# An attention-and-feed-forward kernel on one core: the scaled decay rows of the later blocks move from VectorE to ScalarE, and two small steps change their place

## The chip, the cores and the metric

The kernel runs on one core of one Trainium2 chip. The metric is the device time of one execution in microseconds. The core has engines that run side by side, each through its own instructions in order: PE (TensorE, matrix products, with PEld for its weight loads), DVE (VectorE), ACT (ScalarE), POOL (GpSimd) and SP (SyncE, which here only issues transfers). Transfers are issued by SP, ACT or POOL and carried out by 16 DMA engines. Engines wait for one another through semaphores.

## The reference

Two stages are fused. The first is a state-space attention with a decay per token, over 4 batches, 8 heads, 768 tokens, 32 channels per head and 16 state channels; the second a bilinear feed-forward with 256 model channels and 1536 inner ones.

```python
# per chunk of 32 tokens
cum = np.cumsum(la, axis=-1)                                   # la = log of the decay a
L = np.exp(cum[:, :, :, None] - cum[:, :, None, :]) * causal
y_intra = einsum('bhij,bhjd->bhid', einsum(Cc, Bc) * L, xc)
y_inter = einsum('bhin,bhnd->bhid', Cc, state) * exp(cum)[..., None]
state = exp(sum(la)) * state + sum_j Bx_j * exp(cum[-1] - cum[j])
...
a = x @ w_a; b = x @ w_b                                       # x: tokens x 256
out = (a * b) @ w_out
```

## The kernel before

The sequence is cut into 6 blocks of 128 tokens rather than chunks of 32. A *pair* is one block of two batches, so there are 12 pairs, numbered block by block (0 and 1 are block 0, 2 and 3 block 1, and so on); pairs 0 to 3 are handled one by one ("early", `P0` = 4), the later ones in groups of a block.

**Decays.** `a_sb` holds the decay of the 32 batch-and-head rows by block. `scan` makes `Pr`, the running product of the decay within a block; `over_mid` makes `rmid`, one over the product at the middle token. `Ps` holds `Pr` times `rmid` for the four later blocks (2 to 5). From it come the factors by which B and C are scaled: `late_factors` transposes `Ps` on VectorE into `fCl`, and `spread_rows` copies the last three blocks of `Ps` through DRAM (`rows`, one transfer) into `Pq` (four transfers), from which `block_factors` makes `fCq`. The small steps on `hr`, `hs`, `hsx` turn the decay products into G, the decay that carries the state from one block to the next: a small matrix product with `hsx` (L921) writes it to PSUM and ScalarE copies it out (L924). `maskbd` is a constant mask, cast on ScalarE (L903), that `state_spread` on POOL uses for the states of the pairs 0 and 1.

**Attention of a pair.** B and C are scaled (`scale_bc`), transposed on PE, and multiplied into four PSUM banks (`scores`). VectorE multiplies them by the causal mask for three quarters, and for the fourth, ScalarE copies it to `tmp` (L491) and POOL multiplies (L492). `pv` (or `pv_u` within `group` for the later pairs, matmuls of L500) multiplies the masked scores with x, and the result is copied to X2T or XB.

**Feed-forward.** A `unit(p, k2)` multiplies X2T of a pair by a part of `w_a` (tile `aps`) and of `w_b` (`bps`), ScalarE copies `aps` to `asb` (L711), and `times` on VectorE multiplies `bps` by `asb` into `hk` (L718). `out_mm` multiplies `hk` by `Wo`. Pair 0's first three units are written apart (`units_mm`, tiles `aps` and `bps`, with three `times` behind them); `go` runs units whole.

**What sets the order.** The schedule is written by hand: each engine runs its instructions in the order of the program text, and the framework adds the waits. The feed-forward's products and some others take one of four PSUM banks, in the order of the string `BANKS`: a product has to wait until the last reader of what lay in its bank has finished. Around the change the banks are: `bps` of pair 0's units in 1, 2, 0; unit (1,0) in 3 (`aps`) and 1 (`bps`); unit (1,1) in 3 and 2; unit (1,2) in 0 and 3; then the two `aps` of the units (0,3) and (0,4) in 1 and 0. Transfers issued by SP likewise go out in program order; those behind `spread_rows` are b, c and x of pair 3, then the loads of the later pairs (`loads_bc`, `loads_x`, `load_block`), then the first stores. The four transfers to `Pq` wait until `rows` has landed.

Of the kernel before, what the change touches and what calls it, by code (L numbers as in the profile page):

```python
# [14 lines left out]
ALU = mybir.AluOpType  # L15
# [14 lines left out]
def kernel(  # L30
# [13 lines left out]
    nc = tc.nc  # L44

    nb, H, S, D = x.shape
    N = B.shape[-1]
    Q = 128
# [5 lines left out]
    BH = nb * H  # L54
    NBP = nb // 2
    NP = NBP * NBLK
    NG = NBLK - 1
    P0 = 4
# [22 lines left out]
    headm = ch[:, 0:H]  # L81
# [13 lines left out]
    maskbd = big.tile([128, H, D], f16, name="maskbd")  # L95
    warm = big.tile([128, 128], f16, name="warm")
    causal_q = big.tile([128, Q], f16, name="causal_q")
    Pr = big.tile([BH, NBLK, Q], f32, name="Pr")
    rmid = big.tile([BH, NBLK], f32, name="rmid")
# [5 lines left out]
    NL = NBLK - P0 // NBP  # L105
    Ps = big.tile([BH, NL, Q], f32, name="Ps")
# [31 lines left out]
    def bank(name):  # L138
        return psf.tile([128, 512], f32, name=name, tag=f"ff{next(banks)}")
# [79 lines left out]
    def load_wo(half):  # L219
        return nc.gpsimd.dma_start(  # L220
            Wo[:, 6 * half : 6 * half + 6].rearrange("p (g kk) e -> p g (kk e)", kk=3),
            moe_w_out.rearrange("(g p kk) e -> p g (kk e)", p=128, kk=3)[:, 2 * half : 2 * half + 2],
        )

    nc.sync.dma_start(a_sb, a.rearrange("b h (k q) -> (b h) k q", q=Q))
    for p_ in range(3):
# [22 lines left out]
        out=ident, in_=ident, compare_op=ALU.is_equal, fill=0.0, base=0, pattern=[[-1, 128]], channel_multiplier=1  # L249
    )  # L250
    for bt in range(2):
        v = causal[64 * bt : 64 * bt + 64]
        nc.gpsimd.affine_select(
            out=v, in_=v, compare_op=ALU.is_ge, fill=0.0, base=0, pattern=[[-1, 2], [1, Q]], channel_multiplier=-2
# [26 lines left out]
    def over_mid(lo, hi):  # L281
        nc.vector.reciprocal(rmid[:, lo:hi], Pr[:, lo:hi, 63])
# [33 lines left out]
    def f_c(k):  # L316
        return fC[:, k, H : H + 64].rearrange("p (r b t h) -> p r b t h", r=2, b=NBP, t=2)[:, :, :, 0]

    def late_rows(eng):
        k0 = P0 // NBP  # L320
        eng.tensor_tensor(
            out=Ps, in0=Pr[:, k0:], in1=rmid[:, k0:].unsqueeze(2).broadcast_to((BH, NL, Q)), op=ALU.mult
        )

    def last_factors():
        nc.vector.reciprocal(fBq, fCq[:, NT - 1, :, 0 : 2 * nb])
# [5 lines left out]
    def spread_rows(eng):  # L332
        rows = far.tile([BH, NT, Q], f32, name="rows")
        eng.dma_start(rows, Ps[:, NL - NT :])
        for m in range(4):
            eng.dma_start(
                Pq[32 * m : 32 * m + 2 * nb],
                rows.rearrange("(b h) k q -> b h (k q)", h=H)[:, 2 * m : 2 * m + 2],
            )
# [185 lines left out]
    def ds_mm(p, c0, banks):  # L525
        s = st[p]
        s["DS"] = [b_[:, c0 : c0 + 2 * D] for b_ in banks]
        for bt, m in itertools.product(range(2), range(4)) if p >= P0 else ():
            nc.tensor.matmul(
                s["DS"][bt][32 * m : 32 * m + 32, :],  # L530
                s["bm"][:, bt, 2 * m : 2 * m + 2, :].rearrange("p h n -> p (h n)"),
                by_token(s["X16"])[:, bt, 2 * m : 2 * m + 2].rearrange("p h d -> p (h d)"),
                start=True,
                stop=True,
                skip_group_check=True,
                tile_position=(0, 32 * m),
            )
        for r in range(2) if p < P0 else ():
            for m in range(4):
                for bt in range(2):  # L540
                    k = slice(64 * bt, 64 * bt + 64)
                    nc.tensor.matmul(
                        s["DS"][bt][32 * m : 32 * m + 32, :],
                        s["bm"][k, r, 2 * m : 2 * m + 2, :].rearrange("p h n -> p (h n)"),
                        s["X16"][k, 2 * m : 2 * m + 2, r, :],
                        start=(r == 0),
                        stop=(r == 1),
                        skip_group_check=True,
                        tile_position=(64 * bt, 32 * m),
                    )  # L550
# [92 lines left out]
    def state_sums(p, bts=(0, 1)):  # L643
        blk, bp = divmod(p, NBP)
        for bt in bts:
            g = G[:, 2 * bp + bt, blk : blk + 1]
            ds = st[p]["DS"][bt]
            if blk == 0:
                nc.vector.tensor_scalar(U32[:, p, bt], ds, g, None, ALU.mult)
            else:  # L650
                nc.vector.scalar_tensor_tensor(
                    out=U32[:, p, bt], in0=ds, scalar=g, op0=ALU.mult, in1=gU[:, p % (2 * NBP), bt], op1=ALU.add
                )
# [43 lines left out]
    def units_mm(p, k2s, W, ps, f, ks):  # L697
        for j in ks:
            k2, t_, kk = k2s[j // 2], ps[j // 2], j % 2
            nc.tensor.matmul(  # L700
                t_[:, kk * 2 * Q : (kk + 1) * 2 * Q],
                w_up(W, 2 * k2 + kk, f),
                X2T[:, p, :, f],
                start=(f == 0 and kk == 0),
                stop=(f == 1),
                skip_group_check=True,
            )

    def evac_a(a_ps, on_dve=False):
        asb = ffh.tile([128, 512], f32, name="asb", tag="asb", bufs=5)  # L710
        (nc.vector.tensor_copy if on_dve else nc.scalar.copy)(asb, a_ps)  # L711
        return asb

    def times(p, k2, b_ps, asb):
        s = st[p]
        if "hk" not in s:
            s["hk"] = ffh.tile([128, NK, 2 * Q], f16, name="hk", tag="hk")
        nc.vector.tensor_tensor(  # L718
            out=s["hk"][:, 2 * k2 : 2 * k2 + 2, :].rearrange("p k q -> p (k q)"), in0=b_ps, in1=asb, op=ALU.mult
        )  # L720

    def unit(p, k2, between=None):
        a_ps = unit_mm(p, k2, Wa)
        asb = evac_a(a_ps)
        if between:
            between()
        b_ps = unit_mm(p, k2, Wb)
        return lambda: times(p, k2, b_ps, asb)
# [89 lines left out]
    def fb(k):  # L818
        if k * NBP >= P0:
            nc.vector.reciprocal(fBl[:, 0 : NL - 1], fCl[:, 0 : NL - 1])  # L820
        else:
            nc.vector.reciprocal(fB[:, k], f_c(k))

    def go(*items):
        for p, k2 in items:
            unit(p, k2)()

    def pull(p):
# [33 lines left out]
        out=causal_q, in_=causal_q, compare_op=ALU.is_ge, fill=0.0, base=0, pattern=[[1, Q]], channel_multiplier=-1  # L862
# [18 lines left out]
    asb = [evac_a(aps[0])]  # L881
# [4 lines left out]
    scan(2, 3)  # L886
    scan(5, NBLK)
    over_mid(2, NBLK)
    late_rows(nc.vector)
    spread_rows(nc.sync)  # L890
    for w in range(2):
        for bt in range(2):
            load1(nc.gpsimd, 2, w, bt)
# [1 line left out]
    for bt in range(2):  # L895
        load1(nc.gpsimd, 2, 2, bt)
    tiles(3)
    bps = [bank("bps") for _ in range(3)]
# [1 line left out]
    pv(1)  # L900
    units_mm(0, range(3), Wb, bps, 0, range(4, 6))
    units_mm(0, range(3), Wb, bps, 1, range(6))
    nc.scalar.copy(maskbd, headm.unsqueeze(2).broadcast_to((128, H, D)))  # L903
    times(0, 0, bps[0], asb[0])
    nc.vector.tensor_tensor(out=hr, in0=Pr[:, 0:NG, Q - 1], in1=rmid[:, 0:NG], op=ALU.mult)
    nc.vector.tensor_tensor(out=hs, in0=hr, in1=Pr[:, 1:NBLK, 63], op=ALU.mult)
    nc.vector.tensor_tensor(
        out=hsx[0:BH],
        in0=hs.unsqueeze(1).broadcast_to((BH, nb, NG)),
        in1=selb.rearrange("p (b g) -> p b g", b=nb),  # L910
        op=ALU.mult,
    )
    times(0, 1, bps[1], asb[1])
    times(0, 2, bps[2], asb[2])
    fb(1)
    scale_bc(2, 0, nc.gpsimd)
    scale_bc(2, 1, nc.gpsimd)
    load_wo(1)
    go((1, 0), (1, 1))
    gps = SC[0][:, 256 : 256 + nb * NG]  # L920
    nc.tensor.matmul(gps, indm, hsx.rearrange("p b g -> p (b g)"), start=True, stop=True, skip_group_check=True)  # L921
    for p in range(NBP):
        ds_mm(p, 2 * D * p, SC[:2])
    nc.scalar.copy(G.rearrange("p b g -> p (b g)"), gps)  # L924
    go((1, 2))
    state_sums(0)
    state_sums(1)
# [9 lines left out]
    asb = [evac_a(t_) for t_ in aps]  # L937
# [235 lines left out]
```

## Time and profile before

| what | value |
| --- | --- |
| time, median of 3 runs | 124.03 us (124.01 to 124.08) |
| time of the profiled execution | 123.79 us |
| its span (first to last instruction) | 122.0 us |
| granted TensorE clock, mean | 0.998 |
| PE busy | 117.0 us (96% of the span), 1440 matmuls |
| DVE busy | 93.2 us (76%), 186 instructions |
| ACT busy | 76.4 us (63%), 157 instructions |
| POOL busy | 63.3 us (52%), 86 instructions |
| bytes moved by DMA | 12.25 MB |

Times in the views are microseconds from the start of the span unless marked ns. L12 is line 12 of the kernel; a helper's line stands for all its calls. A timeline row gives start, length, engine, line, operation, the tile written and the tiles read, and how many instructions were merged (x8); in brackets, how long the engine had been idle before and what ended that. In the rows of groups the three fields behind the count are: busy time and mean ns of one; idle time of the engine before them. "SPq" is the issue of a transfer on SP, not its flight. The ends of matmuls are modelled.

### The profile page before, as it was taken

The page shows a single profiled execution, that of the slowest core. Times are in us where ns is not written, and L with a number is a line of the kernel's source. Part 1 is how long each engine was busy: PE and PEld are TensorE (multiplying, and loading weights), DVE is VectorE, ACT ScalarE, POOL GpSimd, SP SyncE. Part 2 cuts the span into 40 slices and gives each one's busy share as a digit, 9 for nine tenths or more (in the row PEclk, how much of TensorE's full clock was granted, in tenths as well). Part 3 has the DMA queues.
Part 4 walks back from the last instruction along what each step waited for, and adds up shares of the span by engine and source line. Part 5 has one row for each costly group of instructions (what it writes and reads, how often), then busy time and mean ns, then how long its engine had stood idle before and what let it go on. Part 6 is the DMA issues. An engine that isn't in the chain of part 4 may idle for free.

```text
span 122.0 us, 3714 instructions
## 1 busy us (share of the span) xinstructions
PE 117.0 (96%) x1440; PEld 79.3 (65%) x1440; DVE 93.2 (76%) x186; ACT 76.4 (63%) x157; POOL 63.3 (52%) x86
## 2 busy tenths in 40 slices
PE   6999899999999999999999999999999999999990
PEld 2345689889898798645476464766464784555890
DVE  4999999895886979699985999996898444847100
ACT  0458856937669865987659657767666737566220
POOL 7997987493883994077998089219044000000000
PEclk9999999999999999999999999999999999999999
DMA  3999999986987297299329961011101012010122
GB/s 62 181 169 207 196 205 209 141 146 84 101 118 121 59 94 130 46 130 131 73 51 206 327 208 43 0 51 43 43 0 43 5 43 86 0 43 5 43 88 84
DMA packets 44593, 12.25 MB, mean 100 GB/s; under 512 B 39296, under 2 KB 44128, under 8 KB 44576
## 3 DMA queue, kind: packets, MB, share of 16 engines
q1 hardware_dynamic: 40000, 7.53, 32.0%
q0 software_dynamic: 2304, 4.06, 17.8%
q10 hardware_dynamic: 2272, 0.43, 1.8%
q8 instruction: 11, 0.18, 0.6%
q14 instruction: 6, 0.05, 0.1%
HBM read 11.18 MB, written 3.19 MB: 118 GB/s over the span
## 4 chain that ended last, share of the span: by engine, by line
PE 86%; DVE 5%; ACT 3%; DMA 2%; issue 1%; DVEq 0%
PE ops L790 18%; PE aps L765 17%; PE bps L765 16%; PE ops L733 9%; PE bps L687 8%; PE aps L687 8%; PE SC L440 2%; DVE t L494 2%; PE SC L500 2%; DMA a_sb<-in_a_dram 2%; PE SC L455 1%; ACT asb L711 1%; PE aps L700 1%; PE tr L406 1%; PE SC L590 1%
## 5 line engine op out<-in xcount | busy, mean ns | idle before, releaser
L711 ACT COPY asb<-aps 128x512 f32<-128x512 f32 x72 | 42.0, 588 | 14.2 <-PE aps L765 9.5
L775 DVE TENSOR_TENSOR hkb<-bps,asb 128x512 f16<-128x512 f32 x48 | 32.0, 687 | 10.5 <-ACT asb L711 10.0
L765 PE MATMUL aps<-XB,Wa 128*128 128x512 f16 x96 | 28.6, 379 | 0.1
L765 PE MATMUL bps<-XB,Wb 128*128 128x512 f16 x96 | 28.5, 379 | 0.0
L790 PE MATMUL ops<-Wo,hkb 128*128 128x256 f16 (+1 forms) x204 | 22.6, 266 | 0.0
L790 PEld LDWEIGHTS <-hkb 128*128 128x128 f16 x204 | 18.5, 98 | 3.0
L494 DVE TENSOR_TENSOR t<-SC,causal_q 128x512 f16<-128x512 f32 x24 | 15.5, 682 | 3.2 <-PE SC L440 3.2
L718 DVE TENSOR_TENSOR hk<-bps,asb 128x512 f16<-128x512 f32 x24 | 15.8, 681 | 2.0 <-ACT asb L711 2.0
L765 PEld LDWEIGHTS <-Wb 128*128 128x128 f16 x96 | 9.9, 103 | 10.9
L492 POOL TENSOR_TENSOR t<-tmp,causal_q 128x512 f16<-128x512 f32 x8 | 9.3, 1159 | 14.5 <-ACT tmp L491 14.2
L765 PEld LDWEIGHTS <-Wa 128*128 128x128 f16 x96 | 9.7, 103 | 9.2 <-issue 0.3
L365 POOL TENSOR_SCALAR x<-xn 128x512 f16<-128x512 f32 x8 | 11.9, 1489 | 3.9 <-DMA xn<-in_x_dram 2.1
L802 ACT ACTIVATE osb<-ops 128x256 f32<-128x256 f32 (+1 forms) x16 | 6.0, 377 | 11.3 <-PE ops L790 11.2
L687 PE MATMUL bps<-X2T,Wb 128*128 128x256 f16 x84 | 12.4, 272 | 0.1
L687 PE MATMUL aps<-X2T,Wa 128*128 128x256 f16 x84 | 12.5, 273 | 0.0
L733 PE MATMUL ops<-Wo,hk 128*128 128x256 f16 x96 | 11.6, 273 | 0.0
L733 PEld LDWEIGHTS <-hk 128*128 128x128 f16 x96 | 9.0, 98 | 1.2
L687 PEld LDWEIGHTS <-Wb 128*128 128x128 f16 x84 | 8.6, 103 | 0.9 <-issue 0.3
L687 PEld LDWEIGHTS <-Wa 128*128 128x128 f16 x84 | 8.3, 104 | 1.1 <-issue 0.2
L494 DVE TENSOR_TENSOR t<-SC,causal 128x512 f16<-128x512 f32 x13 | 8.2, 682 | 0.8 <-PE SC L455 0.6
L491 ACT COPY tmp<-SC 128x512 f32<-128x512 f32 x11 | 6.5, 595 | 1.9 <-PE SC L440 1.1
L267 PE MATMUL SC<-warm 128*128 128x512 f16 (+1 forms) x14 | 5.5, 551 | 1.0 <-POOL warm L238 1.0
(110 smaller groups left out, 136.3 us busy)
## 6 DMA issues: line engine op xcount, KB each, us to landing
out_dram<-osb SPq DMA_DIRECT2D x23, 128.0 KB, 1.7
xn<-in_x_dram SPq DMA_DIRECT2D x5, 256.0 KB, 4.6
Wo<-in_moe_w_out_dram POOLq DMA_DIRECT2D x2, 384.0 KB, 5.4
bn<-in_B_dram SPq DMA_DIRECT2D x6, 128.0 KB, 4.4
rq<-in_C_dram SPq DMA_DIRECT2D x24, 32.0 KB, 2.6
xn<-in_x_dram POOLq DMA_DIRECT2D x3, 256.0 KB, 4.8
Wa<-in_moe_w_a_dram POOLq DMA_DIRECT2D x2, 192.0 KB, 4.9
xn<-in_x_dram SPq DMA_DIRECT2D x3, 128.0 KB, 5.9
```

The costliest lines, as they stand in the source:

```text
L365: eng.tensor_scalar(xo, xi, XS, None, ALU.mult)
L491: nc.scalar.copy(tmp, i_)
L492: nc.gpsimd.tensor_tensor(out=o_, in0=tmp, in1=c_, op=ALU.mult)
L494: nc.vector.tensor_tensor(out=o_, in0=i_, in1=c_, op=ALU.mult)
L687: nc.tensor.matmul(ps[:, kk * 2 * Q : (kk + 1) * 2 * Q], w_up(W, k, f), X2T[:, p, :, f], start=(f == 0), stop=(f == 1), skip_group_check=True,
L711: (nc.vector.tensor_copy if on_dve else nc.scalar.copy)(asb, a_ps)
L718: nc.vector.tensor_tensor(out=s["hk"][:, 2 * k2 : 2 * k2 + 2, :].rearrange("p k q -> p (k q)"), in0=b_ps, in1=asb, op=ALU.mult)
L733: nc.tensor.matmul(o_ps[:, 0:d_model], hk[:, k, bt * Q : (bt + 1) * Q], Wo[:, k, :], start=(k == 0), stop=(k == NK - 1), skip_group_check= ...
L765: nc.tensor.matmul(t_, w_up(W, k, f), XB[:, blk - P0 // NBP, f].rearrange("p t j q -> p (t j q)"), start=(f == 0), stop=(f == 1), skip_gro ...
L775: return lambda: nc.vector.tensor_tensor(out=s["hk"][:, k], in0=ps[1], in1=asb, op=ALU.mult)
L790: nc.tensor.matmul(o_ps[:, 0:w], hk[:, k, c * Q : (c + 1) * Q], Wo[:, k, cs], start=(k == 0), stop=(k == NK - 1), skip_group_check=True,)
L802: nc.scalar.activation(out=o_sb[:, 0:w], in_=o_ps[:, 0:w], func=AF.Copy, scale=1.0 / (YS * YS))
```

## The change

The helper `late_rows` no longer makes all four blocks' rows of `Ps` in one VectorE operation (32x512). It now makes one block's rows at a time (32x128), on ScalarE, by a multiplication with a scale per partition, for the blocks in a given range. Its calls are spread: the rows 1 and 2 where the cast of `maskbd` stood, ahead of the first `times` of pair 0; row 3 between the units (1,0) and (1,1), with `spread_rows` (the SP transfers, which need the rows 1 to 3) right behind it; row 0 behind ScalarE's copy of G. The cast of `maskbd` follows there. On VectorE the second and third `times` of pair 0 come ahead of `hr`, `hs` and `hsx`.

```diff
-    def late_rows(eng):
-        k0 = P0 // NBP
-        eng.tensor_tensor(
-            out=Ps, in0=Pr[:, k0:], in1=rmid[:, k0:].unsqueeze(2).broadcast_to((BH, NL, Q)), op=ALU.mult
-        )
+    def late_rows(lo, hi):
+        for k in range(lo, hi):
+            r = P0 // NBP + k
+            nc.scalar.mul(Ps[:, k], Pr[:, r], rmid[:, r : r + 1])
...
     over_mid(2, NBLK)
-    late_rows(nc.vector)
-    spread_rows(nc.sync)
     for w in range(2):
...
     units_mm(0, range(3), Wb, bps, 1, range(6))
-    nc.scalar.copy(maskbd, headm.unsqueeze(2).broadcast_to((128, H, D)))
+    late_rows(1, 3)
     times(0, 0, bps[0], asb[0])
+    times(0, 1, bps[1], asb[1])
+    times(0, 2, bps[2], asb[2])
     nc.vector.tensor_tensor(out=hr, in0=Pr[:, 0:NG, Q - 1], in1=rmid[:, 0:NG], op=ALU.mult)
...
-    times(0, 1, bps[1], asb[1])
-    times(0, 2, bps[2], asb[2])
     fb(1)
...
     load_wo(1)
-    go((1, 0), (1, 1))
+    go((1, 0))
+    late_rows(3, 4)
+    spread_rows(nc.sync)
+    go((1, 1))
     gps = SC[0][:, 256 : 256 + nb * NG]
...
     nc.scalar.copy(G.rearrange("p b g -> p (b g)"), gps)
+    late_rows(0, 1)
+    nc.scalar.copy(maskbd, headm.unsqueeze(2).broadcast_to((128, H, D)))
     go((1, 2))
```

## The prediction

> **What bounds the kernel now.** I read the page first, then the chain of waits in order of time from 11 to 34 us, then the timeline of all engines over the stretch that the change touches (13.5 to 20.5 us), and last the timelines of the SP and POOL queues, because the change moves a DMA on SP. The page says what ends the kernel:
>
> ```profile
> PE 86%; DVE 5%; ACT 3%; DMA 2%; issue 1%; DVEq 0%
> ```
>
> TensorE is the path, in one chain from about 15 us to the end (PE busy 96%). So a delay of PE anywhere behind 15 us is a delay of the end, and off PE nothing counts until PE waits for it. In the touched stretch the chain reads (start, length, what):
>
> ```profile
> 14.50 0.68 DVE hk L718
> 15.18 0.04 issue
> 15.23 0.60 PE bps L687 x4
> 15.82 0.54 PE aps L687 x4
> 16.36 0.53 PE bps L687 x4
> ```
>
> DVE's first multiplication (`times(0, 0)`) stands on the chain: it frees PSUM bank 1 for the `bps` of unit (1,0). DVE began it only at 14.50, behind the rows that the change takes away. The timeline shows both, and ScalarE beside them:
>
> ```profile
> 13.89 0.68 DVE L321 TENSOR_TENSOR Ps<-Pr,rmid 32x512 f32<-32x512 f32 x1
> 14.31 0.42 ACT L903 CAST maskbd<-ch 128x256 f16<-128x256 f32 x1
> 15.13 0.58 ACT L711 COPY asb<-aps 128x512 f32<-128x512 f32 x1 [0.39 <-PE aps L687]
> ...
> 17.48 0.17 ACT L924 COPY G<-SC 128x20 f32<-128x20 f32 x1 [0.49 <-PE SC L542]
> 17.85 0.58 ACT L711 COPY asb<-aps 128x512 f32<-128x512 f32 x1 [0.20 <-PE aps L687]
> 18.09 1.04 PE L687 MATMUL aps<-X2T,Wa 128*128 128x256 f16 x8
> ```
>
> Here the reader is to see three margins. The copy at 15.13 ends at 15.71, and the next `aps`, in the same bank 3, starts at 15.77. The copy at 17.85, of unit (1,2), ends at 18.43; its bank 0 is wanted by the second half of the eight matmuls at 18.09, that is at 18.53 (four matmuls at 0.109). And between G and that copy ScalarE has 0.20 us to spare.
>
> SP, which the diff touches with one line, has the longest reach:
>
> ```profile
> 14.60 0.32 SPq L334 DMA_DIRECT2D rows<-Ps  x1
> 18.94 3.08 SPq L336 DMA_DIRECT2D Pq<-rows  x4
> 22.12 1.34 SPq L165 DMA_DIRECT2D bn<-in_B_dram  x2
> ...
> 41.65 1.63 SPq L174 DMA_DIRECT2D bn<-in_B_dram  x2
> ```
>
> From 18.94, when `rows` has landed, SP issues without a gap over 0.2 us until 65 us: every load of pairs 3 to 11 but three x stands in line behind `rows`.
>
> **The change, part by part.** Everything is set against the profiled execution: span 122.0, time 123.79, so 1.79 around the span, and 0.24 below the median of 124.03. The differences are added to the median.
>
> *DVE.* The 0.68 of L321 goes, and hr, hs, hsx go behind the third multiplication. `times(0, 0)` then waits only for its matmuls: the eight of L700 start at 13.51, the fourth completes bank 1 at 13.51 + 3 x 0.109 + 0.27 = 14.11, so DVE starts at about 14.15. What PE gets: `bps` of (1,0) at 14.94 (right behind its `aps`, 14.50 + 4 x 0.109) in place of 15.23. This 0.29 is worth nothing, since the next `aps` needs ScalarE's copy (15.71) in any case and starts at 15.77. `bps` of (1,1) waited until 16.30 for the second multiplication and can start at 15.77 + 0.43 = 16.20: **0.10 won**. The matmul with hsx (L921, 16.73 before) would be reached at 16.63; hsx now ends at 14.15 + 3 x 0.63 + 0.54 (from hr's start to hsx's end, 15.10 to 15.64) = 16.58, and a matmul follows DVE by 0.06 (15.17 to 15.23). Just in time.
>
> *ScalarE.* No row shows a 32x128 multiplication by a scale per partition. The nearest are these:
>
> ```profile
> L410 ACT ACTIVATE bt<-SC,ch 128x256 f16<-128x256 f16 x4 | 1.7, 474 | 0.1
> L634 ACT ACTIVATE X2T<-py 128x128 f16<-128x128 f32 x4 | 0.9, 275 | 0.8 <-PE py L515 0.8
> L422 ACT COPY ct<-tr 128x256 f16<-128x256 f16 x2 | 0.8, 377 | 0.0
> L855 ACT COPY fC<-fps 128x32 f32<-128x32 f32 x1 | 0.2, 168 | 0.0
> ```
>
> 128 elements with a fixed scale take 0.275; a scale from a tile adds 0.474 - 0.377 = 0.097 at 256 elements; so 0.37 each, between 0.168 (a quarter of the elements, no scale) and 0.474 (twice the elements). Operations in a row overlap by 0.11 (two of L410 take 0.84, not 0.95). Pieces one and two take the place of the mask's cast: 14.31 + 0.63 = 14.94, before 15.13, free. The third follows the copy of 15.13 and ends at about 15.97, before the next copy at 16.40, free. The fourth and the cast stand between G and the copy of (1,2). G comes 0.10 earlier, at 17.38; 0.17 + 0.37 + 0.42 + 0.58 less three overlaps is 1.21; the copy ends at 18.59 and PE starts at 18.65 instead of 18.53. So **+0.12 at this point**, the 0.10 already in it. Bounds: pieces of 0.168 give -0.08; 0.474 and no overlap at all +0.55.
>
> The Trainium skill ("ScalarE: Activation LUTs", section "What ACT_TABLE_LOAD costs") speaks against cutting one operation in four: a fixed part for every ACTIVATE, 280 ns with an operand per partition, then 0.833 ns for each element, and 93 ns of overlap. By an estimate from it a piece takes 0.387, and this step would be +0.19 rather than +0.12. For 256 elements the same estimate is 0.493, near the 0.474 of L410; no run here shows the piece itself yet.
>
> Behind 18.65 the times of pair 0 and the state sums shift with PE. The state mask is ready near 18.1, its first reader (POOL) runs at 20.82: nothing.
>
> *SP.* `rows` needs pieces one to three, ready at 15.97 rather than 14.57, so it is issued near 16.02: 1.42 later. It landed after 4.3 us, with the DMA engines full (share 1.05 from 15 to 18 us, 1.03 from 18 to 21), and the same load awaits it. Nearest rows for its flight: 2.2 (a_sb, nothing beside it) and 5.6 (c); these bound the delay d of SP's line by -0.7 and +2.7. I take 1.2 for d: 1.42, less 0.2 because the loads of pair 3 then meet less of the second Wo, which lands at 25.1. The four Pq and all that is behind them are d late. Where does that end? Pair 3's c landed at 24.2 + 2.9 = 27.1, and 27.1 + 1.2 + 0.62 (cm on POOL) is 28.9, before PE's 29.34. x of pair 3 (POOL waited for it until 29.99) makes POOL late, but POOL is idle 2.20 before 38.47 and catches up. Then comes the stretch without slack:
>
> ```profile
> 42.12 1.49 POOL L365 TENSOR_SCALAR x<-xn 128x512 f16<-128x512 f32 x1
> 43.69 1.10 POOL L191 TENSOR_TENSOR mq<-rq,fCq 128x512 f16<-128x512 f32 x1
> 44.76 0.62 POOL L376 TENSOR_TENSOR bm<-bn,fBl 128x256 f16<-128x256 f32 x1
> 45.34 1.16 POOL L492 TENSOR_TENSOR t<-tmp,causal_q 128x512 f16<-128x512 f32 x1
> ```
>
> The bn behind `bm` was issued at 41.65; the shortest landing of a bn is 2.9, so it came between 44.55 and 44.76, say 44.65. d late, it holds POOL: the mask of pair 5 (L492) ends at 44.65 + d + 0.58 + 1.16 = 46.39 + d, and PE can read it 0.06 later. PE's L500 (32 matmuls from 46.64, 0.41 to the next line) reads it from the 27th on, at 46.97. So the end is late by 46.45 + d - 46.97 = **d - 0.52** once that exceeds the 0.12, with which it is not added but of which it is the larger. With 1.2: **+0.68**, say 0.67. If the older rq (landed 43.1) limits rather than bn, it is 0.3 less. I find nothing behind that takes it back: PE follows itself there.
>
> Sum: span 122.0 + 0.67 = 122.67; time 124.03 + 0.67 = **124.70**.
>
> **The rivals.**
> *A, the later loads stay hidden.* For it: d under 0.64 suffices, and the flight of `rows` may shorten. Against: the DMA engines are as full at 18 to 21 us as at 15 to 18. Only ScalarE's +0.12 is left: 124.15. The Trainium skill ("DMA: Bandwidth & Descriptors", section "Latency and other measured facts") says that the fixed cost shrinks when HBM is less loaded; that would help A, but the two stretches moved 215 and 204 GB/s.
> *B, faster.* The chain view puts no ScalarE between 15.23 and 15.82. If PE truly waited only for DVE there, the whole 0.29 is won besides the 0.09 at 16.30: -0.38, 123.65. It decides only if d is under 0.5 and the pieces are cheap enough to fit in the spare 0.20. Against it: 15.71 to 15.77 fits the bank exactly.
> *C, later still.* If `rows` meets Wo and x of pair 2 at their worst, d passes 1.6 (27.1 + d + 0.62 + 0.06 beyond 29.34 + 0.12): PE then waits for cm of pair 3 too. At d = 2.0 the lateness is d - 0.52 = 1.48: 125.5.
>
> **How the numbers follow.** Forecast 0.58, A 0.20, B 0.12, C 0.10. A measurement of this kernel tells about 0.2%, 0.25 us, from no change. Faster: B and a little of A, 0.15. Within: most of A and the low end of the forecast (d near 0.7), 0.19. Slower: 0.66. The forecast's own range (d 0.8 to 1.6, with either load as limit) is 124.3 to 125.1; to hold 8 in 10 with A it runs from 123.85 to 125.2, leaving out most of B and C.
>
> **What would show it.** Right: `rows` issued near 16.0, SP's next lines 1 to 1.4 later, POOL idle before `mq` or `bm` near 44 to 46 with a DMA as releaser, PE waiting in L500 for POOL's mask; ScalarE's G, piece, cast and copy in one block from 17.4 to 18.6. Wrong: L500 runs through without a gap, or the `aps` behind 15.23 starts well before 15.77. Should SP's line catch up before 41 us, the forecast falls to A.

## The result, and the profile after

| | before | after |
| --- | --- | --- |
| time, median of 12 runs each | 124.00 us (123.87 to 124.09) | 124.83 us (124.18 to 126.09) |
| profiled execution: time, span | 123.79, 122.0 us | 124.84, 123.1 us |
| PE busy | 117.0 us (96%) | 117.2 us (95%) |
| ACT instructions | 157 | 161 |

The changed kernel is slower: 1.0066 times the time of before, 95% interval 1.0048 to 1.0084. A second set of runs of the same kernel gave 1.0058 (1.0036 to 1.0079). Executions more than 1.5% above the fastest of their kernel are left out of the ratios and of the spreads given in the text. The changed kernel's times spread over 1.3 us (1.9 with its longest, 126.09), those of before in the same set over 0.22, but in the later sets over 0.9 to 1.7.

The shares of the chain that ended last, from the page of the changed kernel:

```profile
PE 83%; DMA 7%; DVE 3%; ACT 3%; issue 1%; DVEq 0%; ACTq 0%
```

PE still is the chain. Most of the 7% of DMA is the landing of Wb (6.18 us of the chain, up to 13.09), which lies ahead of everything that was changed. What is new is a second place of ScalarE on it, behind G; the chain of waits of the changed kernel, in order of time (start, length, what):

```profile
15.56 0.59 ACT asb L710
16.15 0.04 issue
16.20 0.60 PE aps L686 x4
...
18.00 0.03 ACT G L924
18.03 0.04 issue
18.07 0.33 ACT Ps L322
18.40 0.27 issue
18.67 0.58 ACT asb L710
```

The first three rows are the wait that the prediction put between 15.23 and 15.77: DVE is gone from it, and ScalarE's copy is what holds the next `aps`. The rest is the block of G, piece, cast and copy; PE's `aps` follows it at 19.29. The 0.27 of "issue" is the mask's cast, which runs in it.

SP's line in the changed kernel, from its timeline:

```profile
16.46 0.32 SPq L333 DMA_DIRECT2D rows<-Ps  x1
20.62 2.78 SPq L335 DMA_DIRECT2D Pq<-rows  x4
23.51 1.34 SPq L165 DMA_DIRECT2D bn<-in_B_dram  x2
...
42.90 1.73 SPq L174 DMA_DIRECT2D bn<-in_B_dram  x2
```

Against the rows of before, `rows` is 1.86 late, the bn of pair 3 1.39, the last one 1.25. POOL behind it:

```profile
46.01 0.62 POOL L375 TENSOR_TENSOR bm<-bn,fBl 128x256 f16<-128x256 f32 x1
46.59 1.16 POOL L491 TENSOR_TENSOR t<-tmp,causal_q 128x512 f16<-128x512 f32 x1
```

POOL's mask of pair 5 ends at 47.75 instead of 46.50, and yet PE does not wait for it: PE is later still. To see where PE became late, I set the start of each matmul against that of the same matmul in the profile of before, and list the places where the difference steps (time in the profile of before; us; the changed kernel's two profiled executions, spans 123.1 and 122.7):

| place | first | second |
| --- | --- | --- |
| ahead of the change (to 14.5: loads of the start, mostly Wb's landing) | +0.42 | +0.08 |
| 15.23 `bps` of (1,0), given back at 15.77 | -0.15, +0.15 | -0.27, +0.27 |
| 16.30 `bps` of (1,1) | -0.10 | -0.09 |
| 16.7 the matmul with hsx | +0.19 | +0.08 |
| 18.53 second `aps` behind G | +0.24 | +0.24 |
| 30.86 `scores` of pair 3 | +0.33 | +0.33 |
| 47.00 27th matmul of L500 | none | none |
| total at the last matmul | +1.08 | +0.63 |

The step at 30.86 was not in the prediction at all. ScalarE's timeline there, in the kernel before:

```profile
28.99 0.38 ACT L745 ACTIVATE osb<-ops 128x256 f32<-128x256 f32 x1 [0.27 <-PE ops L733]
29.48 0.59 ACT L711 COPY asb<-aps 128x512 f32<-128x512 f32 x1
```

and in the kernel after:

```profile
29.75 0.38 ACT L744 ACTIVATE osb<-ops 128x256 f32<-128x256 f32 x1 [0.27 <-PE ops L732]
30.58 0.59 ACT L710 COPY asb<-aps 128x512 f32<-128x512 f32 x1 [0.44 <-PE SC L405]
```

The copy of unit (2,0) follows the evacuation of `osb` by 0.49 before and by 0.83 after. The bracket names PE, but the record of ScalarE's own wait shows that it was passed 0.39 before the copy began; elsewhere a copy begins 0.056 behind such a wait. So ScalarE stood 0.33 with nothing to wait for that the profile shows. Counted in the built program, waits included, this copy is ScalarE's 65th instruction after the change. Before, the 65th was the copy of unit (2,1). It too began 0.39 behind its wait, but two `bt` operations kept ScalarE busy until 0.11 before its start, so the delay was hidden.

### The profile page after: what moved, and what is told of

Read it like the earlier page. It is cut to its first block, busy times and chain, and to the rows that moved or that the text cites. A ratio compares the mean times of both kernels' runs of the same rounds, so it can differ in the third digit from the quotient of the medians.

```text
span 123.1 us, 3719 instructions
## 1 busy us (share of the span) xinstructions
PE 117.2 (95%) x1440; PEld 79.3 (64%) x1440; DVE 92.6 (75%) x185; ACT 77.6 (63%) x161; POOL 63.3 (51%) x86
## 4 chain that ended last, share of the span: by engine, by line
PE 83%; DMA 7%; DVE 3%; ACT 3%; issue 1%; DVEq 0%; ACTq 0%
PE ops L789 17%; PE aps L764 17%; PE bps L764 16%; PE ops L732 9%; PE aps L686 7%; PE bps L686 6%; DMA Wb<-in_moe_w_b_dram 5%; PE SC L439 2%; ACT asb L710 2%; PE SC L499 2%; DMA a_sb<-in_a_dram 2%; PE bps L699 1%; PE tr L405 1%; PE SC L514 1%; PE SC L589 1%
## 5 line engine op out<-in xcount | busy, mean ns | idle before, releaser
L732 PE MATMUL ops<-Wo,hk 128*128 128x256 f16 x96 | 11.6, 273 | 0.0
```

The lines of the kernel that those rows point to most:

```text
L732: nc.tensor.matmul(o_ps[:, 0:d_model], hk[:, k, bt * Q : (bt + 1) * Q], Wo[:, k, :], start=(k == 0), stop=(k == NK - 1), skip_group_check= ...
```

## The experiments

In the quoted texts, theory 1 is SP's late line; theory 2 says that only ScalarE's block behind G costs; theory F is a fixed cost on entering ScalarE's 65th instruction. "Steps" are the differences of PE's starts as in the table above.

### The changed kernel again

No edit.

> The changed kernel unaltered, for a second profile and more times. Theory 1 (SP's line of loads is late and pair 3's cm or a later load is waited for): times again spread over more than 1 us, median near 124.8, and the profile shows POOL waiting for a DMA between 27 and 31 us or near 45 us, with PE late behind it. Theory 2 (only ScalarE's block behind G costs): the lateness against before is about 0.3 and no more, so most of the rest would be a DMA landing ahead of the change (Wb near 13 us), and this second profile need not show it.

Measured: 124.50 us (124.30 to 125.49), before 123.88 (123.58 to 124.55), ratio 1.0058 (1.0036 to 1.0079). Its steps are the second column above. The steps at 18.53 and 30.86 repeat to 0.01 us, while SP's line does not: its last bn was 0.40 late here and 1.25 in the first profile. In this set the times of the changed kernel spread over 1.19 us and those of before over 0.97.

### Only the rows late

Before, with the transfer of `rows` held until VectorE's second multiplication; nothing else is changed.

```diff
...
-    spread_rows(nc.sync)
...
-    times(0, 1, bps[1], asb[1])
+    t01 = times(0, 1, bps[1], asb[1])
+    r_ = spread_rows(nc.sync)
+    tc.add_manual_dep(r_.ins, t01.ins.name, AFTER, reason="rows late")
```

> The kernel before, in which the rows transfer alone waits for VectorE's second multiplication (ends at 16.2 us), so it is issued some 1.6 us late and nothing else is moved. Theory 1: SP's line is 1.3 to 1.7 late, POOL waits for cn of pair 3 near 28 us, time +0.3 to +1.0 and a spread of about 1 us. Theory 2: the loads stay hidden, 124.0 within 0.1 and as steady as the kernel before.

Measured: 124.87 us (124.05 to 126.24), ratio 1.0067 (1.0036 to 1.0097). The profiled execution is the longest of them, with a granted clock of 0.996, so its rows are read for places and not for sizes. From POOL's timeline:

```profile
29.20 0.62 POOL L377 TENSOR_TENSOR bm<-bn,fB 128x256 f16<-128x256 f32 x1 [2.55 <-DMA bn<-in_B_dram]
30.73 0.62 POOL L377 TENSOR_TENSOR cm<-cn,fC 128x256 f16<-128x256 f32 x1 [0.92 <-DMA cn<-in_C_dram]
```

`rows` was issued at 16.22 and took until 22.4. POOL waits for pair 3's b and c, PE waits for POOL (steps of 0.62 and 1.41 at 29.2 and 29.3), and once more at the 27th matmul of L500 (0.40). So a late `rows` alone makes the kernel slower, in this one profile at the places of the forecast and of rival C, by 0.2 to 1.8 us in the other nine executions (124.05 to 125.72 against 123.88).

### The transfers to Pq behind pair 3's loads

The changed kernel, with the four transfers to `Pq` issued behind the b, c and x of pair 3.

```diff
...
-    spread_rows(nc.sync)
+    rows = spread_rows(nc.sync)
...
     loads_x(3, nc.sync)
+    spread_back(nc.sync, rows)
     loads_bc(4)
```

> The changed kernel, in which the four Pq transfers go behind pair 3's loads in SP's line, so b, c and x of pair 3 no longer wait for rows to land; the later pairs' loads then come no later than in the kernel before. Theory 1: the wait for cm of pair 3 goes and the spread with it; 124.2 to 124.4. Theory 2: the same time as the changed kernel, 124.8.

Measured: 124.51 us (124.26 to 125.92), ratio 1.0059 (1.0035 to 1.0083). Pair 3's loads did not come earlier: their first bn was issued at 22.94 (23.51 and 22.82 in the two profiles of the changed kernel). Steps: +0.19 at 16.7, +0.24 at 18.53, +0.33 at 30.86, and +0.25 at the 27th matmul of L500. The run did not separate the theories, but its profile shows the predicted hold: POOL waited 0.56 for the rq and 0.18 for the bn just ahead of that mask.

### ScalarE's block taken apart

The changed kernel, with the fourth piece and the cast behind unit (1,2).

```diff
     nc.scalar.copy(G.rearrange("p b g -> p (b g)"), gps)
+    go((1, 2))
     late_rows(0, 1)
     nc.scalar.copy(maskbd, headm.unsqueeze(2).broadcast_to((128, H, D)))
-    go((1, 2))
```

> The changed kernel, in which the fourth piece and the mask's cast go behind the copy of unit (1,2), so that G's copy is followed at once by that copy. Theory 1: 0.1 to 0.4 is won (the ScalarE block) but the late loads remain, 124.4 to 124.7, spread still about 1 us. Theory 2: back to 124.0 to 124.1 and steady.

Measured: 124.25 us (124.00 to 125.31), ratio 1.0030 (1.0009 to 1.0052). The step at 18.53 is gone, those at 16.7 (+0.19) and 30.86 (+0.34) are there. From its timeline of ScalarE:

```profile
17.44 0.18 ACT L924 COPY G<-SC 128x20 f32<-128x20 f32 x1 [0.58 <-PE SC L541]
17.82 0.58 ACT L710 COPY asb<-aps 128x512 f32<-128x512 f32 x1 [0.20 <-PE aps L686]
```

The copy follows G by 0.38, as before (17.48 to 17.85), and not by 0.67. This order recovers 0.24 us in the profile and 0.25 in the medians (124.50 to 124.25, whose intervals overlap).

### Four small copies more on ScalarE: what moves the 65th instruction

Before, with four copies of 32x1 near 19.5 us, where ScalarE has time; the changed order is not in it. The first kernel writes into a new small tile, the second into `warm`, which nothing reads any more.

```diff
+    spare = big.tile([BH, 8], f32, name="spare")
...
     asb = [evac_a(t_) for t_ in aps]
+    for i in range(4):
+        nc.scalar.copy(spare[:, i : i + 1], Pr[:, 0, i : i + 1])
```

> The kernel before with four copies of 32x1 added on ScalarE in its idle time near 19.5 us, into a tile that nothing reads; all else is unchanged, no wait and no load is moved. Theory F (a place in ScalarE's own instruction stream, the 65th instruction, is entered late by 0.3 to 0.4 us; four instructions more ahead of it put the copy of aps of unit (2,0) there, on PE's path): PE steps back by 0.30 to 0.35 at pair 3's scores near 30.9 us and nowhere else, time 124.1 to 124.3. Rival (the step at the scores comes from cm or x of pair 3 arriving late): no step, 123.9.

> The kernel before with four copies of 32x1 on ScalarE near 19.5 us, this time into the tile warm, which is no longer read, so that no tile is added and none moves its address. Theory F: the one step of 0.34 at pair 3's scores remains, and the times are steadier than with the added tile: 124.15 to 124.3, spread under 1 us. Rival (the added instructions make loads late by themselves): holds at 47.0 us again, median 124.7.

Measured, with the new tile: 124.70 us (124.11 to 126.10), ratio 1.0051 (1.0028 to 1.0075), steps +0.33 at 30.86 and +0.99 at the 27th matmul of L500. Into `warm`: 124.19 us (124.03 to 124.67), ratio 1.0026 (1.0012 to 1.0040), +0.34 in all behind 16.3, reached at 30.9 (0.18 of it already at 29.3, where POOL had idled 1.47 for pair 3's cn; ScalarE's copy comes later than that and contains it). The copy of unit (2,0) in the second kernel (timeline of ScalarE):

```profile
29.76 0.58 ACT L711 COPY asb<-aps 128x512 f32<-128x512 f32 x1 [0.45 <-PE SC L406]
```

`osb` was evacuated from 28.93, so it is the same 0.83 to the copy as after the change. Four instructions more, here at another place than in the changed kernel, are enough for it, and it costs some 0.3 us, with little spread. In the first kernel a hold of SP's line came on top, though `rows` is issued at 14.59 as before; what the tile itself did is told in the last section.

### Two copies more: the place moved on

The changed kernel and the one with the block apart, each with two such copies, so that the 65th instruction falls on an evacuation of `osb`.

```diff
     asb = [evac_a(t_) for t_ in aps]
+    for i in range(2):
+        nc.scalar.copy(spare[:, i : i + 1], Pr[:, 0, i : i + 1])
```

> The changed kernel and the two copies of 32x1 on ScalarE. Theory F: the step at 30.9 us goes and the one at 18.5 us (0.24) stays, so 124.1 to 124.3 where no load is waited for; since PE is then earlier, the predicted hold at 47.0 us (the 27th matmul of L499) may come out, 0.1 to 0.4, in some executions. Rival: 124.5 to 124.8 as the changed kernel.

> The kernel with the block apart (fourth piece and cast behind the copy of (1,2)) and two such copies of 32x1 on ScalarE near 19.5 us. Theory F: the 65th instruction is then one between two long waits, the step of 0.34 at 30.9 us goes, 123.85 to 124.0. Rival (late loads): the step stays, 124.25 or a little above.

Measured: 124.75 us (124.03 to 125.69), ratio 1.0068 (1.0041 to 1.0095), and 124.72 us (123.93 to 127.49), ratio 1.0049 (1.0025 to 1.0072). In both profiles the step at 30.86 is gone, which supports theory F; the first keeps the +0.24 at 18.53, the second does not. But the medians did not fall; in the first profile PE was 0.87 late already at 14.5, ahead of every edit. Both kernels hold the new tile, and the last section says what came with it. The profile of the second shows what took the place; POOL's timeline:

```profile
45.78 0.62 POOL L376 TENSOR_TENSOR bm<-bn,fBl 128x256 f16<-128x256 f32 x1 [0.70 <-DMA bn<-in_B_dram]
46.36 1.17 POOL L492 TENSOR_TENSOR t<-tmp,causal_q 128x512 f16<-128x512 f32 x1
```

PE's timeline in the same kernel:

```profile
46.81 0.57 PE L500 MATMUL SC<-t,x 128*32 128x128 f16 x26
47.58 0.29 PE L500 MATMUL SC<-t,x 128*32 128x128 f16 x6 [0.20 <-POOL t L492]
```

This is the hold of the forecast, to the matmul: POOL idles for the bn, its mask ends at 47.53, and PE stops after 26 of the 32 matmuls, +0.41.

### SP's late line alone

The kernel with the block apart and two copies into `warm`: the steps at 18.53 and 30.86 are gone and no tile is added. In a second one hr, hs and hsx also stand between the second and third multiplication.

```diff
     times(0, 1, bps[1], asb[1])
-    times(0, 2, bps[2], asb[2])
     nc.vector.tensor_tensor(out=hr, in0=Pr[:, 0:NG, Q - 1], in1=rmid[:, 0:NG], op=ALU.mult)
...
+    times(0, 2, bps[2], asb[2])
     fb(1)
```

> The changed kernel with the block apart and two such copies into warm: ScalarE's block and the 65th instruction are both out of PE's way, and SP's line is as late as in the changed kernel (rows issued near 16.1 us). Theory 1 (the late line costs by itself): some executions held at 47.0 us or at cm of pair 3; median 124.0 to 124.5 and a spread of 1 us or more. Rival (the block and the 65th instruction are all of the lateness): 123.9, as steady as the kernel before.

> The same with hr, hs and hsx between the second and the third multiplication, so that L921 need not wait for hsx: PE 0.10 to 0.25 earlier from 16.8 us on, 0.1 to 0.2 below apart_fill2w; a kernel under 123.87 only if the late line costs nothing.

Measured: 124.57 us (123.69 to 125.92, 8 runs), ratio 1.0029 (0.9999 to 1.0059), and 124.45 us (123.64 to 126.27), ratio 1.0021 (0.9987 to 1.0055), with before at 123.91 (123.61 to 125.76). The best executions are as fast as before's best, the others up to 1.7 us longer. The first profile holds PE by +0.41 at pair 3's `cm` (POOL idle 1.35 for its cn), the second by +0.20 there, +0.39 at the 27th matmul of L500, and by +1.03 at pair 2's `cm`, whose load POOL issues ahead of all that was edited. The intervals are wide, and the before of this set had a spread of its own; the late line's own cost is not settled to better than 0 to 0.6%.

### VectorE's order alone

Before, with the second `times` ahead of hr, hs and hsx, and the third behind them.

```diff
     times(0, 0, bps[0], asb[0])
+    times(0, 1, bps[1], asb[1])
     nc.vector.tensor_tensor(out=hr, in0=Pr[:, 0:NG, Q - 1], in1=rmid[:, 0:NG], op=ALU.mult)
...
-    times(0, 1, bps[1], asb[1])
     times(0, 2, bps[2], asb[2])
```

> The kernel before with one edit on VectorE: the second multiplication of pair 0 ahead of hr, hs and hsx (the third stays behind them). Theory: the bps of unit (1,1) starts at 16.20 instead of 16.30 and hsx is still in time for L921, so 0.10 is won and kept: 123.75 to 123.85. Rival: given back at the next copy of ScalarE, 123.88 as before.

Measured: 123.86 us (123.71 to 124.79), ratio 1.0000 (0.9983 to 1.0017). The profile has the -0.10 at 16.30, and no step at the matmul with hsx takes it back. But three kernels in which VectorE still has the order of before show the same -0.09 or -0.10 there: the one with the late rows and both with four small copies. In these three VectorE began its second multiplication 0.02 to 0.14 earlier than in the profile of before and PE came 0.03 to 0.12 later, so PE did not have to wait, without any edit of VectorE's order. So the profile does not show that this edit won anything, and 0.1 us is under what the times can tell: no version here is shown to be faster than before.

### SP's step alone undone

The changed kernel, with the rows 1 to 3 made by VectorE and sent by SP where they were before; ScalarE's pieces remain, three of them writing into `warm`.

```diff
...
     over_mid(2, NBLK)
+    nc.vector.tensor_tensor(
+        out=Ps[:, 1:], in0=Pr[:, 3:], in1=rmid[:, 3:].unsqueeze(2).broadcast_to((BH, NT, Q)), op=ALU.mult
+    )
+    spread_rows(nc.sync)
...
     late_rows(3, 4)
-    spread_rows(nc.sync)
```

> The changed kernel with SP's step alone undone: VectorE makes the rows 1 to 3 of Ps ahead of pair 0's first multiplication, as before, and rows is issued there; the three pieces of ScalarE stay where they are but write into an unused part of `warm`, so that ScalarE's instructions keep their number and their places. VectorE is then late again for hsx. Theory 1 (SP's late line makes the spread and the long executions, ScalarE the steady part): rows issued near 14.5, bn of pair 3 near 22.1, no hold of PE at pair 3's cm or at the 27th matmul of L500; the steps at the aps behind G (0.15 to 0.3) and at pair 3's scores (0.34) stay; the lowest time stays at about 0.5 to 0.7 over the kernel before's lowest, the median 0.5 to 0.7 over its median, and lowest and highest lie within 0.8. Rival S (the spread comes from ScalarE's or VectorE's new order): times from 0.4 to 2 above the kernel before, as in the changed kernel, with rows issued early all the same.

Measured: 124.32 us (123.99 to 125.17), before 124.11 (123.64 to 125.85), ratio 1.0022 (0.9995 to 1.0049). The step at 18.53 is there (+0.24), and no hold at pair 3's `cm` or in L500. The step at 30.86 is not, against what was expected: writing into `warm` added one wait to ScalarE's instructions, ahead of the first piece, and the 65th instruction became the wait ahead of the copy instead of the copy. In its timeline the evacuation of `osb` began at 29.92 and the copy at 30.41, so it follows by 0.49 as before the change, with no idle time marked: one place decides it. On the spread the run is inconclusive: 1.18 us instead of the 0.8 expected, but before spread over 1.22 in this set. PE was 0.60 late already at 14.5 in this profile.

## Why the prediction was right, point by point

The total and its direction came out as forecast: +0.83 and +0.62 us in the medians of two sets, forecast +0.67. The sum behind it was not the one that the profiles show, so that the size agrees is luck.

- *What bounds the kernel.* Right. Each step of PE in the table is found again in the span (1.08 of 1.09, 0.63 of 0.66).
- *The 0.29 at 15.23 is worth nothing.* Right: PE came 0.15 and 0.27 earlier, and all of it was given back at 15.77, where the chain shows ScalarE's copy. Rival B falls with it.
- *0.10 won at 16.30, hsx just in time.* The 0.10 shows in both profiles, but it is not safely the change's: kernels with VectorE's order of before show it too (under VectorE's order alone), so the wait at 16.30 belongs to the one execution from which it was read. In the first profile it would have gone in any case: PE was 0.42 late ahead of the change, VectorE's scan only 0.13. The second is wrong: the matmul with hsx came 0.19 and 0.08 late, and took back more than the 0.10 in the first profile and nearly all of it in the second. The chain of three multiplications, 1.89, was as computed. VectorE began it at 14.76 and 14.29; the L700 matmuls that it waits for were 0.53 and 0.07 late, so that is 14.23 and 14.22 instead of 14.15. With hsx ahead of the third multiplication no such step is seen.
- *ScalarE's block behind G.* Right in place and mechanism. From G to the end of the copy: 1.25 and 1.24, computed 1.21. A piece took 0.40 (computed 0.37), two 0.68, the cast 0.39. For the piece the estimate from the Trainium skill ("ScalarE: Activation LUTs", "What ACT_TABLE_LOAD costs"), 0.387, was nearer. For the step it was not: without the 0.10 at 16.30 the prediction's sum is 0.22, the estimate's 0.29, and 0.24 was measured. The net of the stretch was +0.22 in the second profile (-0.10, +0.08, +0.24) and +0.34 in the first, in place of +0.12, for the most part by the lateness of hsx. With the block apart its +0.24 was gone.
- *SP: d = 1.2, the end held at the 27th matmul of L500 by d - 0.52 = 0.68.* This step, the largest term of the sum, failed in size: it measured nothing. L500 ran through without a gap in both profiles of the changed kernel, which is the prediction's own sign of being wrong. `rows` was issued at 16.46 and 16.11, forecast 16.02. But d at the last bn was 1.25 in one profile and 0.40 in the other. The 27th matmul starts at 47.00 in the trace of before, not at 46.97. In the first the formula gives 0.73 against the kernel before, and PE was by then 1.10 late from other causes, so that the mask, ready at about 47.81 for a matmul due at 47.00 + 1.10 = 48.10, was covered by 0.29. POOL itself ran 1.10 late there (its `mq` began at 44.79 instead of 43.69) and stood only 0.12 idle ahead of `bm`. In the second, d is below 0.52. The mechanism itself is real: five other kernels show PE held at exactly this matmul, by 0.25 to 0.99, and rival C's place, pair 3's `cm`, held PE in four. But in each of the two groups one kernel issues `rows` on time (those with four small copies; the one that is held in L500 also has the added tile), so loads can be late without a late `rows`, which takes away what covers them. It is a cost that one execution pays and the next does not; as a fixed 0.68 it was wrong. Whether it makes the wider spread of times stays open. The late rows alone gave 124.05 to 125.72 against 123.58 to 124.55, but part of the scatter lies ahead of all edits: at 14.5 us PE was 0.42, 0.60 and 0.87 late in three of the profiles (the first of the changed kernel, SP's step undone, the changed kernel with two copies) and between -0.13 and +0.19 in the other ten. What makes the three late is not known.
- *What was missing.* +0.33 at pair 3's scores, from four more instructions ahead of ScalarE's 65th. Together with the late hsx it took the place of the SP term, and so the sum agreed, by luck.

Put together from the runs, in per cent of 124 us: block and hsx 0.22 (SP's step undone), the 65th instruction 0.26 (four copies into `warm`), 0.48 or 0.60 us together; 0.10 to 0.18 more in the changed kernel remain for SP's line and for what the intervals leave open. This split is an estimate: the interval of the 0.22 alone runs from -0.05 to 0.49, and with the block apart, where `rows` is issued at 15.90, the whole of 0.30 is about what hsx (0.09 us net) and the 65th instruction give.

## What to carry to other kernels

On the engine that feeds the critical one, count the instructions and not only their time: four that fit in idle time still moved a delay from a place where it was hidden to a copy that PE waits for. A load that hangs on a moved result has no single lateness: price it by its range over executions, and against how late the engine that waits for it already is. A sum that agrees with the total proves none of its terms; set the starts of the critical engine's instructions of both traces against each other, and each term shows at its place.

## What the runs showed of the hardware

**The 65th instruction of ScalarE.** In all nine profiles in which a copy is the 65th, it begins 0.39 us behind its passed wait: on unit (2,0)'s copy in the changed kernel twice, with the Pq transfers behind, with the block apart and in both kernels with four copies; on unit (2,1)'s in before, with the late rows and with VectorE's order alone. In the five in which the 65th is an evacuation or a wait ahead of unit (2,0)'s copy, that copy begins 0.056 to 0.057 behind its wait. A packet of 8 KB on the instruction queue q14 moves along: it starts at 30.5 to 32.1 us where the 65th is a copy of unit (2,0) or (2,1) (34.2 with the late rows), at 27.0 to 28.4 where it is earlier. It starts 0.65 to 1.35 us behind the delayed copy, so it is not what that copy waits for. That it is the entry into a new block of instructions is argued from this and not shown. The Trainium skill ("Runtime: NRT & Kernel Launch", section "Instruction fetch mechanics") describes refills in blocks of 256 instructions whose crossing is mostly hidden; here the place is the 65th, and the cost was hidden or 0.33 us, by what stood there.

**An added tile of 32 bytes per partition** slowed the small packets of SP's queue: over 20 to 70 us, packets of 64 bytes took 10.8 ns on average in all the kernels without it and 11.6 to 12.0 with it; those of 128 bytes 12.9 to 13.0 and 14.9 to 15.3; the medians are the same. The tile moves the addresses of those behind it: in the built programs the tiles that these loads fill (bn, cn, xn, rq) start at multiples of 64 bytes without it and 32 bytes off one with it. That this is the reason is not shown. With the same copies into `warm` the times spread over 0.64 us instead of 1.32; that is one comparison, from two sets of runs.
